# Four one-bank accumulators for dispatch, and the last batch's g in two chunk buffers

## The chip, the core and the metric

The kernel runs on one NeuronCore of a Trainium2 chip. The metric is the device time of one execution in microseconds (us), median of several runs. Of the core, TensorE (PE in the rows, PEld its weight loads), VectorE (DVE), ScalarE (ACT), GpSimd (POOL) and SyncE (SP) have queues of their own and wait for each other by semaphores; SP issues every DMA, in the order of its queue.

## The reference, cut to what matters

```python
def reference(q, k, v, moe_w_in, moe_w_out, phi, w1, w2):
    # q, k, v: (4, 12, 448, 64); causal softmax attention, per batch and head
    x = attention(q, k, v).transpose(0, 2, 1, 3).reshape(1792, 768)
    h = x @ moe_w_in                       # 768 x 2048, float64 weights
    g = np.maximum(0.01 * h, h)
    y = g @ moe_w_out                      # 2048 x 768
    logits = y @ phi                       # 1792 x 32: 8 experts of 4 slots
    d = softmax(logits, axis=0)            # dispatch: over all 1792 tokens
    slot_input = d.T @ y                   # 32 x 768
    for e in range(8):                     # w1[e]: 768 x 1024, w2[e]: 1024 x 768
        slot_out[4*e : 4*e+4] = relu(slot_input[4*e : 4*e+4] @ w1[e]) @ w2[e]
    c = softmax(logits, axis=1)            # combine
    return c @ slot_out                    # 1792 x 768, float32
```

## The kernel before, in words

Tokens are worked on in four batches of 448. Attention and the first layer are pipelined over stages: while the attention of batch b runs, `up(b - 1)` (L650) makes the 16 column tiles of g (128 of the 2048 columns each, `H` in PSUM, then `g` in SBUF) of the batch before it, and the float64 weights are converted. y is never formed: dispatch is taken as (d.T @ g) @ w_out, with w_out converted to float32 in a DRAM scratch (`wsc`), and the logits as g @ (w_out @ phi), `wprime`.

**Dispatch over batches.** The softmax over all tokens is kept running. `combine(b)` (L733) takes a batch's logits: `lt` and `pl` on PE, the new maximum `nm`, the factor `ab` by which all earlier sums shrink, `et` = exp, its transpose `dn`; then the accumulator `g_acc` (128 x 4 x 512 in PSUM, four banks, x = 0 to 3) is multiplied by `ab`, bank by bank, banks 0 and 2 on DVE, 1 and 3 on ACT (L765 to L768), and 56 calls of `mm` (L792; 112 instructions in the trace, as float32 goes in two passes) add dn.T @ g_nat. `g_nat` holds one batch's g with tokens on partitions, made by 32 x 32 transposes on DVE (`transpose_g`, L629). The batches come in the order 2, 0, 1, 3. Batch 2 goes through during stage four and only starts the accumulator, so it has nothing to rescale. Batches 0 and 1 were parked in DRAM (`g_far`) and come back through `fetch` (L710, `gb`), while `up(3)` runs; batch 3 is combined last.

**The expert weights.** `slots` (L860) is a list of places of 12 KB per partition, taken round after round by `load_next` (L891); 36 chunks of 1.5 MB go through them in this order: 4 of `wo` (from `wsc`), 16 of `w1`, 16 of `w2`. The names count down: `wo_35` to `wo_32`, `w1_31` to `w1_16`, `w2_15` to `w2_0`. The places are buffers that fall free late: 7 `wg` (the fetch buffers of batches 0 and 1), 4 `wq` (first-layer weights w16, four f each), 2 `wx` (x16 of batches 2 and 3, of which one also holds `g_spare`, batch 3's g for f < 6), and 3 `wc`, which lie where `mainp` (g_nat and batch 3's ring of five g tiles) was: 13 loads are asked for before the last combine (L908) and 3 behind it (L915). From then on each load waits until PE has used up the chunk 16 places earlier (`load_next(1)` behind each chunk's products).

**The end.** Behind the last `g_acc`: `ge` (normalised), `pgt`, `psi` (the four wo chunks), `pst`, `ph` (w1), `po` (w2), `pss`, and the output `o`. The order on each engine is set by a scheduler that works on a simulated timeline; PE's matmuls keep the written order (`in_order`, L102).

Of the kernel before, what the change touches and what calls it, by code (L numbers as in the profile page):

```python
# [10 lines left out]
F32 = mybir.dt.float32  # L11
# [23 lines left out]
def tile_attn_moe_softmoe(ctx: ExitStack, tc: tile.TileContext, q, k, v, w_in, w_out, phi, w1, w2, out, dbg=None):  # L35
# [17 lines left out]
    const = ctx.enter_context(tc.tile_pool(name="const", bufs=1))  # L53
    xpool = tc.alloc_tile_pool(name="xpool", bufs=2)
    wpool = ctx.enter_context(tc.tile_pool(name="wpool", bufs=1, side="right"))
# [15 lines left out]
    run_s = const.tile([128, 1], F32, name="run_s")  # L71
    w16 = [wpool.tile([128, 2, NP, 512], F16, name=f"w16_{i}", tag="wq", bufs=4) for i in range(4)]

# [412 lines left out]
    def columns(n):  # L486
# [15 lines left out]
        if hp == 0:  # L502
            x16[b] = xpool.tile([128, CHUNK // 2], F16, tag="x16", name=f"x16_{b}")[:, : NP * 2 * S].rearrange(
                "p (c x s) -> p c x s", c=NP, x=2
            )
# [119 lines left out]
    g_nat = None  # L625
    g_acc = [None]
    l4s = {}
# [22 lines left out]
    def up(b, before=()):  # L650
# [4 lines left out]
        if b == B - 1:  # L655
            spare = xpool.tile([128, CHUNK // 4], F32, tag="x16", name="g_spare")
        iv[b] = const.tile([128, NF], F32, tag="iv", bufs=2, name=f"iv{b}")
# [7 lines left out]
        for f in range(NF):  # L665
# [17 lines left out]
            if not far and not before and f >= group + 5:  # L683
                logits(b, group)
                group += 4
            if b == B - 1 and f < NSPARE:
                g = spare[:, S * f : S * (f + 1)]
            else:
                g = mainp.tile([128, S], F32, tag="g", bufs=GBUF if b > 1 else 3, name=f"g{b}_{f}")
            gts[b, f] = g  # L690
# [42 lines left out]
    def combine(b):  # L733
# [7 lines left out]
        def s1():  # L741
# [19 lines left out]
            if b == 2:  # L761
                nc.vector.tensor_copy(run_s, sb)
            else:
                for x in range(4):
                    if x % 2:  # L765
                        scalar.activation(g_acc[0][:, x], g_acc[0][:, x], AF.Copy, scale=ab)
                    else:
                        nc.vector.tensor_scalar(g_acc[0][:, x], g_acc[0][:, x], ab, None, ALU.mult)  # L768
            dn = mainp.tile([128, S // 32, NS], F32, tag="dn", name=f"dn{b}")
            nc.vector.transpose(dn, et.rearrange("p (c x) -> p c x", x=32))  # L770
            if b != 2:
                nc.vector.scalar_tensor_tensor(run_s, run_s, ab, sb, ALU.mult, ALU.add)
            m = const.tile([CP, NI], F32, tag="cm", bufs=1, name=f"cm{b}")
            cs = c_nat[:, NI * b : NI * (b + 1)]
            nc.vector.tensor_reduce(m, pl, AX.X, ALU.max)
            nc.vector.tensor_tensor(cs, pl, m.unsqueeze(2).to_broadcast([CP, NI, NS]), ALU.subtract)
            st.update(dn=dn)

        def s3():
            cs = c_nat[:, NI * b : NI * (b + 1)]  # L780
            scalar.activation(cs, cs, AF.Exp)
# [6 lines left out]
        def s4():  # L788
            dn, acc = st["dn"], g_acc[0]
            nb = S // 32  # L790
            for c in range(nb):
                o = 32 * (c % 4)  # L792
                for x in range(4):
                    r = slice(32 * x, 32 * x + 32)
                    mm(
                        acc[o : o + 32, x], dn[r, c], g_nat[r, c], start=b == 2 and c < 4, stop=c >= nb - 4,
                        skip_group_check=True,
                    )
# [26 lines left out]
    if True:  # L825
# [11 lines left out]
        TR[0] = 2  # L837
        mainp = tc.alloc_tile_pool(name="gring", bufs=1, reuse_waits="tile")
        pools[1] = tc.alloc_tile_pool(name="conv2", bufs=1, reuse_waits="tile")
        load_raw()  # L840
        fixed[0] = True
        for b in range(1, 4):
            if b == 3:
                tc_release(pools[1])
                tc_release(mainp)
                mainp = tc.alloc_tile_pool(name="mainp", bufs=1, reuse_waits="tile")
                pools[2] = tc.alloc_tile_pool(name="conv", bufs=1, side="right", reuse_waits="tile")
                load_raw()
                g_nat = mainp.tile([128, S // 32, DFF // 4], F32, name="g_nat")
# [7 lines left out]
        wa[0] = tc.alloc_tile_pool(name="wa", bufs=1, side="right", reuse_waits="tile")  # L857
        NQ, NX, NC = 4, 2, 3
        wc = [None]
        slots = ["wg"] * (NG - 1) + ["wq"] * NQ + ["wx"] * NX + ["wg"] + ["wc"] * NC  # L860

# [21 lines left out]
        def slot(shape, name, dtype=F32):  # L883
            where = slots[taken[0] % len(slots)]
            taken[0] += 1
            pool, tag, bufs = {
                "wg": (wa[0], "wg", NG), "wq": (wpool, "wq", NQ), "wx": (xpool, "x16", NX), "wc": (wc[0], "wc", NC),
            }[where]
            return pool.tile(list(shape), dtype, tag=tag, bufs=bufs, name=name)
# [14 lines left out]
        HB[0], TR[0] = 2, 2  # L904
        g_acc[0] = psum.tile([128, 4, 512], F32, name="g_acc")
        for _ in up(B - 1, combine(B - 2) + late):
            pass
        load_next(NQ + NG + NX)  # L908
        for step in combine(B - 1):
# [13 lines left out]
        for x in range(4):  # L923
            ge = fin.tile([128, 512], F32, tag="ge", bufs=2, name=f"ge{x}")
            if x % 2:
                nc.scalar.activation(ge, g_acc[0][:, x], AF.Copy, scale=run_s)
            else:
                nc.vector.tensor_scalar(ge, g_acc[0][:, x], run_s, None, ALU.mult)
            for k in range(4):
# [136 lines left out]

    for p in (fin, psum2, wc[0], wa[0], xpool):
        tc_release(p)
# [44 lines left out]
```

## Time and profile before

| what | value |
|---|---|
| median of 3 runs | 666.31 us (664.75 to 669.99) |
| profiled execution | 664.25 us, its span 662.3 us |
| mean granted clock of TensorE | 0.959 |
| PE busy | 582.0 us (88% of the span) |
| DVE / ACT / POOL busy | 366.6 / 291.4 / 235.5 us |
| DMA | 125.67 MB, mean 190 GB/s |

The span runs from the first to the last instruction; 1.95 us of the profiled time lie around it. Busy shares are averages over stages with different limits: the attention stages end at about 435 us, dispatch at 552 us, and the experts at 642 us.

### The profile page before, as it was taken

To read this page: it belongs to the slowest core of one execution; us is meant where nothing else is said; L and a number is where in the kernel's file an instruction comes from. 1 tells how busy PE (TensorE), PEld (TensorE's weight loads), DVE (VectorE), ACT (ScalarE), POOL (GpSimd) and SP (SyncE) were. 2 spreads that over 40 slices of the span, in tenths; PEclk is the share of its full clock that TensorE was granted. 3 is DMA by queue.
4 is the path that set the end of the run, shared out by engine and by line. 5 is a ranking of instruction groups with operands and counts; after the bars stand their busy time and mean duration, and the time that the engine had idled before them with its cause. 6 is when DMAs were issued, how large, how long until landed. Compare 5 with 4: busy or idle time off the path is not lost.

```text
span 662.3 us, 12288 instructions
## 1 busy us (share of the span) xinstructions
PE 582.0 (88%) x4836; PEld 329.6 (50%) x4836; DVE 366.6 (55%) x884; ACT 291.4 (44%) x571; POOL 235.5 (36%) x247
## 2 busy tenths in 40 slices
PE   3788889998999999999999999999989968997654
PEld 2456555554555655665555555543434434553124
DVE  5868668989955666654567566346365241001014
ACT  2677655776864656665456455411202120011013
POOL 5287952587784335542334444320000000000000
PEclk9799989998999999999999999999989997899698
DMA  9941346665642556643253222049974546999968
GB/s 186 281 117 43 84 115 175 180 165 139 196 107 76 156 179 207 187 119 95 66 142 109 84 65 81 25 157 322 349 298 179 190 191 246 423 421 424 426 253 333
DMA packets 102449, 125.67 MB, mean 190 GB/s; under 512 B 69240, under 2 KB 91256, under 8 KB 98296
## 3 DMA queue, kind: packets, MB, share of 16 engines
q1 hardware_dynamic: 102392, 124.89, 57.2%
q8 instruction: 38, 0.62, 0.4%
q14 instruction: 19, 0.16, 0.1%
HBM read 105.74 MB, written 19.14 MB: 189 GB/s over the span
## 4 chain that ended last, share of the span: by engine, by line
PE 60%; DMA 11%; DVE 10%; POOL 8%; ACT 6%; issue 3%; SPq 1%; ACTq 0%; POOLq 0%; DVEq 0%
PE H L102 26%; DMA w<-in_moe_w_dram 9%; PE O L102 5%; PE T L102 5%; PE g_acc L102 3%; PE dn L102 3%; PE S L102 2%; DVE g_nat L632 2%; PE qkps L102 2%; PE ph L971 2%; PE L L102 2%; DMA raw_i_None<-in_moe_w_in_dram 2%; PE wt_ps L102 2%; POOL w L245 2%; ACT P L113 2%
## 5 line engine op out<-in xcount | busy, mean ns | idle before, releaser
L102 PE MATMUL H<-x,w 128*128 128x448 f16 x1152 | 230.7, 355 | 0.7 <-ACT g L113 0.7
L102 PEld LDWEIGHTS <-w 128*128 128x128 f16 x1152 | 111.2, 99 | 112.4 <-issue 19.6
L396 DVE CUSTOM_DVE_ANT_0 junk<-S,mask 112x224 bf16<-112x224 f32 (+3 forms) x192 | 85.1, 443 | 60.2 <-PE S L102 57.2
L113 ACT ACTIVATE g<-H,iv 128x448 f32<-128x448 f32 x58 | 36.8, 634 | 104.2 <-PE H L102 81.1
L474 DVE RECIPROCAL rs<-rs 128x224 f32<-128x224 f32 x36 | 53.4, 1524 | 40.3 <-ACT rs L113 40.3
L113 ACT ACTIVATE P<-T 112x672 f32<-112x672 f32 (+1 forms) x72 | 56.9, 792 | 21.9 <-PE T L102 20.8
L436 POOL TENSOR_SCALAR_AFFINE_SELECT P<-P 112x448 f32<-112x448 f32 x48 | 31.0, 647 | 90.6 <-ACT P L113 53.6
L102 PE MATMUL T<-qkt 64*112 64x336 f32 (+3 forms) x576 | 59.4, 318 | 4.3 <-ACT P L113 3.2
L102 PE MATMUL O<-P,v 112*64 112x448 f32 (+3 forms) x384 | 53.2, 418 | 4.5 <-POOL P L436 4.4
L102 PEld LDWEIGHTS T<-qkt 64*112 64x112 f32 x576 | 42.2, 177 | 14.3 <-issue 5.7
L445 POOL TENSOR_TENSOR tsum<-tsum,P 112x448 f32<-112x448 f32 (+1 forms) x48 | 47.3, 986 | 1.9
L1059 PE MATMUL po<-w,hz 128*32 128x384 f32 x256 | 28.4, 566 | 16.3 <-DMA w<-in_moe_w_dram 16.3
L102 PEld LDWEIGHTS O<-P,v 112*64 112x64 f32 x384 | 25.7, 140 | 29.9 <-issue 12.6
L963 POOL MEMSET hz<- 128x256 f32 x2 | 0.6, 311 | 111.1 <-PE g_acc L102 111.1
L441 POOL TENSOR_TENSOR tsum<-P 112x672 f32<-112x672 f32 x24 | 39.1, 1630 | 1.8
L102 PE MATMUL S<-qkt 64*112 64x224 f32 (+3 forms) x192 | 31.5, 368 | 8.4 <-DVE mxe L396 3.7
L374 DVE TENSOR_TENSOR qkt<-qkps,qkt 128x448 fp32r<-128x448 f32 x48 | 29.1, 621 | 10.0 <-ACT qkt L113 10.0
L632 DVE STREAM_TRANSPOSE g_nat<-g 128x448 f32<-128x448 f32 x26 | 16.5, 638 | 30.2 <-ACT g L113 30.2
L102 PE MATMUL T<-mr,onesr 64*112 64x448 f32 (+1 forms) x192 | 30.6, 314 | 2.9 <-ACT mr L113 2.9
L236 POOL TENSOR_TENSOR cv_i_None<-cv_i_None,cs_i_None 128x768 f32<-128x768 f32 x16 | 28.6, 1785 | 11.0 <-ACT cs_i_None L113 11.0
L113 ACT ACTIVATE mr<-mps,own 128x112 fp32r<-128x112 f32 x96 | 26.2, 360 | 14.0 <-PE mps L102 13.9
L113 ACT COPY rs<-dn 128x448 f32<-128x448 f32 x18 | 9.6, 532 | 50.3 <-PE dn L102 50.3
(174 smaller groups left out, 878.6 us busy)
## 6 DMA issues: line engine op xcount, KB each, us to landing
w<-in_moe_w_dram SPq DMA_DIRECT2D x32, 1536.0 KB
raw_i_None<-in_moe_w_in_dram SPq DMA_DIRECT2D x16, 768.0 KB
raw_o_None<-in_moe_w_out_dram SPq DMA_DIRECT2D x10, 768.0 KB
g_far<-g SPq DMA_DIRECT2D x32, 224.0 KB
gb<-g_far SPq DMA_DIRECT2D x8, 896.0 KB
wo<-wsc SPq DMA_DIRECT2D x4, 1536.0 KB
qk<-in_q_dram SPq DMA_DIRECT2D x48, 112.0 KB
qk<-in_k_dram SPq DMA_DIRECT2D x48, 112.0 KB
```

The lines of the kernel that those rows point to most:

```text
L102: op(*args, **kwargs)
L113: op(*args, **kwargs)
L236: nc.gpsimd.tensor_tensor(t, t, sg, ALU.mult)
L245: nc.gpsimd.tensor_tensor(lo, w, hi, ALU.subtract)
L374: nc.vector.tensor_tensor(st[:, j, 1], p, st[:, j, 0].bitcast(F32), ALU.subtract)
L396: nc.vector.tensor_tensor_reduce(out=junk[:, :w], in0=ps[:, a, at : at + w], in1=mask[:, S - w :], scale=-1.0, scalar=3e38, op0=ALU.add, o ...
L436: nc.gpsimd.affine_select(out=d, in_=d, compare_op=ALU.is_ge, fill=0.0, base=0, pattern=[[0, 4], [1, CP]], channel_multiplier=-1,)
L441: nc.gpsimd.tensor_tensor(tsum[:CP], p[0][:CP, :, 0, CP:], p[0][:CP, :, 1, : S - CP], ALU.add)
L445: nc.gpsimd.tensor_tensor(y, y, p[1][:CP, :, j, : S - CP * (j + 2)], ALU.add)
L474: nc.vector.reciprocal(rs[:, c : c + S // 2], rs[:, c : c + S // 2])
L632: nc.vector.transpose(g_nat[:, :, 32 * f : 32 * (f + n)].rearrange("p c (f x) -> p f c x", x=32), gts[b, f].rearrange("p (c x) -> p c x", ...
L1059: nc.tensor.matmul(po[h][32 * g : 32 * g + 32], hp[:, (t0 + t) % 8], wt[:, t, DH * h - c0 : DH * (h + 1) - c0], start=t0 + t < 4, stop=t0 ...
```

## The change

`g_acc` becomes four tiles of one bank each (`g_acc0` to `g_acc3`). In `combine`, the row maximum and subtraction for the second softmax (`cm`, `c_nat`) are written in `s3`, behind the products, instead of `s1`. The ring of g tiles gets a pool of its own (`gring2` in stage four), which is released before `up(3)`; all 16 g tiles of batch 3 lie in two chunk buffers instead, f < 6 in `g_spare0` (a new place, `wd`), the others in `g_spare1` (`wq0`, where w16 of f < 4 was), six columns of tiles, used again from f = 12. x16 no longer gives one of its two buffers to g, so `wx0` is free as soon as batch 2 is through. Each of the `wq` and `wx` buffers has a tag of its own. The places are now 1 `wx0`, 7 `wg`, `wq1`, `wd`, `wq2`, `wq3`, `wx1`, `wq0` and 2 `wc`: 14 loads before the last combine and 2 behind it, still 16 in all.

```diff
-    xpool = tc.alloc_tile_pool(name="xpool", bufs=2)
+    xpool = tc.alloc_tile_pool(name="xpool", bufs=1)
-    w16 = [wpool.tile([128, 2, NP, 512], F16, name=f"w16_{i}", tag="wq", bufs=4) for i in range(4)]
+    w16 = [wpool.tile([128, 2, NP, 512], F16, name=f"w16_{i}", tag=f"wq{i}") for i in range(4)]
...
-            x16[b] = xpool.tile([128, CHUNK // 2], F16, tag="x16", name=f"x16_{b}")[:, : NP * 2 * S].rearrange(
+            x16[b] = xpool.tile([128, CHUNK // 2], F16, tag=f"wx{b % 2}", name=f"x16_{b}")[:, : NP * 2 * S].rearrange(
...
         if b == B - 1:
-            spare = xpool.tile([128, CHUNK // 4], F32, tag="x16", name="g_spare")
+            spares.append(wd[0].tile([128, CHUNK // 4], F32, tag="wd", name="g_spare0"))
...
-            if b == B - 1 and f < NSPARE:
-                g = spare[:, S * f : S * (f + 1)]
+            if b == B - 1:
+                if f == NSPARE:
+                    spares.append(wpool.tile([128, CHUNK // 4], F32, tag="wq0", name="g_spare1"))
+                g = spares[f >= NSPARE][:, S * (f % NSPARE) : S * (f % NSPARE + 1)]
             else:
-                g = mainp.tile([128, S], F32, tag="g", bufs=GBUF if b > 1 else 3, name=f"g{b}_{f}")
+                g = ring[0].tile([128, S], F32, tag="g", bufs=GBUF if b > 1 else 3, name=f"g{b}_{f}")
...
                 for x in range(4):
                     if x % 2:
-                        scalar.activation(g_acc[0][:, x], g_acc[0][:, x], AF.Copy, scale=ab)
+                        scalar.activation(g_acc[x], g_acc[x], AF.Copy, scale=ab)
                     else:
-                        nc.vector.tensor_scalar(g_acc[0][:, x], g_acc[0][:, x], ab, None, ALU.mult)
+                        nc.vector.tensor_scalar(g_acc[x], g_acc[x], ab, None, ALU.mult)
...
                     mm(
-                        acc[o : o + 32, x], dn[r, c], g_nat[r, c], start=b == 2 and c < 4, stop=c >= nb - 4,
+                        g_acc[x][o : o + 32], dn[r, c], g_nat[r, c], start=b == 2 and c < 4, stop=c >= nb - 4,
...
         wa[0] = tc.alloc_tile_pool(name="wa", bufs=1, side="right", reuse_waits="tile")
-        NQ, NX, NC = 4, 2, 3
+        tc_release(ring[0])
+        wd[0] = tc.alloc_tile_pool(name="wd", bufs=1, side="right", reuse_waits="tile")
+        NC = 2
         wc = [None]
-        slots = ["wg"] * (NG - 1) + ["wq"] * NQ + ["wx"] * NX + ["wg"] + ["wc"] * NC
+        slots = ["wx0"] + ["wg"] * NG + ["wq1", "wd", "wq2", "wq3", "wx1", "wq0"] + ["wc"] * NC
...
-        g_acc[0] = psum.tile([128, 4, 512], F32, name="g_acc")
+        g_acc += [psum.tile([128, 512], F32, name=f"g_acc{x}") for x in range(4)]
         for _ in up(B - 1, combine(B - 2) + late):
             pass
-        load_next(NQ + NG + NX)
+        load_next(len(slots) - NC)
...
-                nc.scalar.activation(ge, g_acc[0][:, x], AF.Copy, scale=run_s)
+                nc.scalar.activation(ge, g_acc[x], AF.Copy, scale=run_s)
```

How the change moves instructions, at three places.

VectorE's queue in `combine(0)` (the rescalings are the rows that write g_acc), before:

```order
L776 TENSOR_TENSOR c_nat<-pl_5515,cm_5537 112x128
L755 TENSOR_TENSOR ab_5522<-nm_5520,run_m 128x1
L757 COPY run_m<-nm_5520 128x1
L770 STREAM_TRANSPOSE dn_5534<-et_5527 128x448
L783 TENSOR_REDUCE cs_5622<-c_nat 112x4
L768 TENSOR_SCALAR g_acc<-g_acc,ab_5522 128x512
L772 SCALAR_TENSOR_TENSOR run_s<-run_s,ab_5522,sb_5528 128x1
L784 TENSOR_SCALAR cs_5622<-cs_5622 112x4
L785 RECIPROCAL cs_5622<-cs_5622 112x4
L786 TENSOR_TENSOR c_nat<-c_nat,cs_5622 112x128
L768 TENSOR_SCALAR g_acc<-g_acc,ab_5522 128x512
```

and now:

```order
L785 TENSOR_TENSOR c_nat<-pl_5525,cm_5628 112x128
L760 TENSOR_TENSOR ab_5532<-nm_5530,run_m 128x1
L762 COPY run_m<-nm_5530 128x1
L775 STREAM_TRANSPOSE dn_5544<-et_5537 128x448
L788 TENSOR_REDUCE cs_5632<-c_nat 112x4
L773 TENSOR_SCALAR g_acc_5321<-g_acc_5321,ab_5532 128x512
L773 TENSOR_SCALAR g_acc_5323<-g_acc_5323,ab_5532 128x512
L777 SCALAR_TENSOR_TENSOR run_s<-run_s,ab_5532,sb_5538 128x1
L789 TENSOR_SCALAR cs_5632<-cs_5632 112x4
L790 RECIPROCAL cs_5632<-cs_5632 112x4
L791 TENSOR_TENSOR c_nat<-c_nat,cs_5632 112x128
```

The second rescaling (its row is the one with g_acc that stood last, behind c_nat) now follows the first at once. The subtraction from `pl`, which the diff writes into `s3`, stands ahead of `dn` in both, so that edit moves nothing here. Batch 1's and batch 3's combines have changed in the same way.

ScalarE's queue at the same place, before:

```order
L113 ACTIVATE c_nat<-c_nat 112x128
L113 ACTIVATE ab_5522<-ab_5522 128x1
L113 ACTIVATE g_acc<-g_acc,ab_5522 128x512
L113 ACTIVATE g_spare<-H_4_5541,iv_5316 128x448
L113 ACTIVATE g_acc<-g_acc,ab_5522 128x512
L113 ACTIVATE g_spare<-H_5_5617,iv_5316 128x448
```

and now:

```order
L113 ACTIVATE c_nat<-c_nat 112x128
L113 ACTIVATE ab_5532<-ab_5532 128x1
L113 ACTIVATE g_acc_5322<-g_acc_5322,ab_5532 128x512
L113 ACTIVATE g_acc_5324<-g_acc_5324,ab_5532 128x512
L113 ACTIVATE g_spare_5325<-H_4_5548,iv_5326 128x448
L113 ACTIVATE g_spare_5325<-H_5_5624,iv_5326 128x448
```

The two rescalings of ACT stand together, directly behind `ab`; the g of f = 4, which stood between them, comes behind.

SP's queue at the first chunk loads, before:

```order
L715 DMA gb6_5308<-g_far_103 128x4x448
L715 DMA gb7_5452<-g_far_103 128x4x448
L897 DMA wo_35_6016<-wsc_104 128x4x768
L897 DMA wo_34_6018<-wsc_104 128x4x768
L897 DMA wo_33_6020<-wsc_104 128x4x768
L897 DMA w1_29_6028<-in_moe2_w1_dram 128x3072
L897 DMA wo_32_6022<-wsc_104 128x4x768
L897 DMA w1_31_6024<-in_moe2_w1_dram 128x3072
```

and now:

```order
L720 DMA gb6_5315<-g_far_103 128x4x448
L906 DMA wo_35_6017<-wsc_104 128x4x768
L720 DMA gb7_5462<-g_far_103 128x4x448
L906 DMA wo_34_6019<-wsc_104 128x4x768
L906 DMA wo_33_6021<-wsc_104 128x4x768
L906 DMA wo_32_6023<-wsc_104 128x4x768
L906 DMA w1_31_6025<-in_moe2_w1_dram 128x3072
L906 DMA w1_30_6027<-in_moe2_w1_dram 128x3072
```

`wo_35` goes ahead of the last fetch (into `wx0`), and `w1_29` (place `wq0`, early) has left this stretch. The last loads ahead of and behind the last combine (`w1_22` to `w1_20` were the three of `wc`), before:

```order
L897 DMA w1_27_6032<-in_moe2_w1_dram 128x3072
L897 DMA w1_26_6034<-in_moe2_w1_dram 128x3072
L897 DMA w1_24_6038<-in_moe2_w1_dram 128x3072
L897 DMA w1_22_6135<-in_moe2_w1_dram 128x3072
L897 DMA w1_21_6137<-in_moe2_w1_dram 128x3072
L897 DMA w1_20_6139<-in_moe2_w1_dram 128x3072
L897 DMA w1_19_6186<-in_moe2_w1_dram 128x3072
```

and now:

```order
L906 DMA w1_25_6037<-in_moe2_w1_dram 128x3072
L906 DMA w1_24_6039<-in_moe2_w1_dram 128x3072
L906 DMA w1_23_6041<-in_moe2_w1_dram 128x3072
L906 DMA w1_22_6043<-in_moe2_w1_dram 128x3072
L906 DMA w1_21_6138<-in_moe2_w1_dram 128x3072
L906 DMA w1_20_6140<-in_moe2_w1_dram 128x3072
L906 DMA w1_19_6187<-in_moe2_w1_dram 128x3072
```

The names stand in nearly the same order; what differs is the place that each load takes. `w1_22` takes `wq0`, free when batch 3's last g tile has been transposed and its logits taken, and only `w1_21` and `w1_20` take `wc`.

## Rows read from the trace of the kernel before

**Rows 1.** Page, part 2: busy tenths of the DMA engines, 40 slices.

```profile
DMA  9941346665642556643253222049974546999968
```

**Rows 2.** Stretches: us, busy us by engine, granted clock, DMA share, GB/s.

```profile
510.00:530.00 20.00, 20.00 (x115) 9.43 (x112) 6.69 (x13) 3.17 (x6) 0.00 (x0) 1.00 0.43 157
530.00:550.00 20.00, 14.32 (x135) 6.59 (x146) 6.91 (x20) 3.60 (x8) 0.00 (x0) 0.84 0.40 159
575.00:600.00 25.00, 25.00 (x360) 13.18 (x348) 3.66 (x18) 2.69 (x7) 1.07 (x4) 1.00 1.01 422
```

**Rows 3.** Chain of waits from 545 us: start us, us, what.

```profile
582.39 28.76 DMA w<-in_moe_w_dram
611.21 29.51 DMA w<-in_moe_w_dram
640.76 1.50 PE po L1059 x16
```

**Rows 4.** Timeline of SP: start us, us, line, operation, xcount.

```profile
536.18 0.80 SPq L897 DMA_DIRECT2D w<-in_moe_w_dram  x2
552.03 1.28 SPq L897 DMA_DIRECT2D w<-in_moe_w_dram  x3
560.51 13.19 SPq L897 DMA_DIRECT2D w<-in_moe_w_dram  x7
```

**Rows 5.** Short stretches behind an issue, columns as in rows 2.

```profile
552.00:552.50 0.50, 0.00 (x1) 0.00 (x0) 0.39 (x1) 0.00 (x0) 0.43 (x2) 1.00 0.00 0
552.50:553.00 0.50, 0.09 (x1) 0.09 (x1) 0.36 (x1) 0.10 (x1) 0.13 (x1) 1.00 0.15 25
```

**Rows 6.** Timeline, batch 0's combine: start us, us, ... [idle before <-releaser].

```profile
470.94 3.57 PE L102 MATMUL H<-x,w 128*128 128x448 f16 x18
472.44 0.19 ACT L113 ACTIVATE ab<-ab 128x1 f32<-128x1 f32 x1
473.11 0.74 DVE L768 TENSOR_SCALAR g_acc<-g_acc,ab 128x512 f32<-128x512 f32 x1
473.89 0.66 ACT L113 ACTIVATE g_acc<-g_acc,ab 128x512 f32<-128x512 f32 x1 [1.25 <-DVE g_acc L768]
474.58 0.76 DVE L768 TENSOR_SCALAR g_acc<-g_acc,ab 128x512 f32<-128x512 f32 x1
475.37 0.66 ACT L113 ACTIVATE g_acc<-g_acc,ab 128x512 f32<-128x512 f32 x1 [0.19 <-DVE g_acc L768]
476.09 4.33 PE L102 MATMUL g_acc<-g_nat,dn 32*32 32x512 f32 x112 [1.58 <-ACT g_acc L113]
```

**Rows 7.** Waits of PE from 440 to 552 us: total, times, longest.

```profile
PE g_acc L102 <- ACT g_acc L113: 8.1, 3, 5.0
PE L L102 <- DVE l L646: 3.5, 2, 2.0
```

**Rows 8.** Timeline of DVE behind batch 0's products.

```profile
480.46 8.06 DVE L632 STREAM_TRANSPOSE g_nat<-gb 128x896 f32<-128x896 f32 x8 [5.12 <-PE g_acc L102]
```

**Rows 9.** Timeline, the last logits and batch 3's combine.

```profile
536.08 1.73 PE L102 MATMUL L<-g,wprime 128*32 128x448 f32 x8
542.25 0.75 DVE L768 TENSOR_SCALAR g_acc<-g_acc,ab 128x512 f32<-128x512 f32 x1
545.23 6.77 PE L102 MATMUL g_acc<-g_nat,dn 32*32 32x512 f32 x112 [4.96 <-ACT g_acc L113]
```

**Rows 10.** PE at batch 2's products, which wait for no rescaling.

```profile
450.61 4.33 PE L102 MATMUL g_acc<-g_nat,dn 32*32 32x512 f32 x112
```

**Rows 11.** Stretches around the last products, columns as in rows 2.

```profile
540.30:543.70 3.40, 0.00 (x0) 0.00 (x0) 3.02 (x14) 1.68 (x5) 0.00 (x0) 1.00 0.98 411
547.10:550.60 3.50, 3.50 (x82) 1.67 (x66) 0.00 (x0) 0.00 (x0) 0.00 (x0) 0.50 0.00 0
```

**Rows 12.** Timeline: ACT and DVE both reading PSUM.

```profile
529.25 0.63 ACT L113 ACTIVATE g<-H,iv 128x448 f32<-128x448 f32 x1 [3.64 <-PE L L102]
529.33 0.62 DVE L648 TENSOR_TENSOR l<-L,l 128x448 f32<-128x448 f32 x1 [3.04 <-PE L L102]
```

More of the change, by code (lines that the diff above doesn't have):

```diff
@@ L625, in tile_attn_moe_softmoe @@
     g_nat = None
-    g_acc = [None]
+    g_acc = []
+    ring = [None]
+    wd = [None]
+    spares = []
     l4s = {}
@@ L772, in s1, with s3 @@
                 nc.vector.scalar_tensor_tensor(run_s, run_s, ab, sb, ALU.mult, ALU.add)
+            st.update(dn=dn, pl=pl)
+        def s3():
+            pl = st["pl"]
             m = const.tile([CP, NI], F32, tag="cm", bufs=1, name=f"cm{b}")
@@ L776, in s1 @@
             nc.vector.tensor_tensor(cs, pl, m.unsqueeze(2).to_broadcast([CP, NI, NS]), ALU.subtract)
-            st.update(dn=dn)
-        def s3():
-            cs = c_nat[:, NI * b : NI * (b + 1)]
             scalar.activation(cs, cs, AF.Exp)
@@ L788, in s4 @@
         def s4():
-            dn, acc = st["dn"], g_acc[0]
+            dn = st["dn"]
             nb = S // 32
@@ L837, in tile_attn_moe_softmoe @@
         TR[0] = 2
-        mainp = tc.alloc_tile_pool(name="gring", bufs=1, reuse_waits="tile")
+        ring[0] = tc.alloc_tile_pool(name="gring", bufs=1, reuse_waits="tile")
         pools[1] = tc.alloc_tile_pool(name="conv2", bufs=1, reuse_waits="tile")
@@ L844, in tile_attn_moe_softmoe @@
                 tc_release(pools[1])
-                tc_release(mainp)
+                tc_release(ring[0])
                 mainp = tc.alloc_tile_pool(name="mainp", bufs=1, reuse_waits="tile")
+                ring[0] = tc.alloc_tile_pool(name="gring2", bufs=1, reuse_waits="tile")
                 pools[2] = tc.alloc_tile_pool(name="conv", bufs=1, side="right", reuse_waits="tile")
@@ L857, in tile_attn_moe_softmoe @@
         wa[0] = tc.alloc_tile_pool(name="wa", bufs=1, side="right", reuse_waits="tile")
-        NQ, NX, NC = 4, 2, 3
+        tc_release(ring[0])
+        wd[0] = tc.alloc_tile_pool(name="wd", bufs=1, side="right", reuse_waits="tile")
+        NC = 2
         wc = [None]
-        slots = ["wg"] * (NG - 1) + ["wq"] * NQ + ["wx"] * NX + ["wg"] + ["wc"] * NC
+        slots = ["wx0"] + ["wg"] * NG + ["wq1", "wd", "wq2", "wq3", "wx1", "wq0"] + ["wc"] * NC
         chunks = []
@@ L886, in slot @@
             pool, tag, bufs = {
-                "wg": (wa[0], "wg", NG), "wq": (wpool, "wq", NQ), "wx": (xpool, "x16", NX), "wc": (wc[0], "wc", NC),
-            }[where]
+                "wg": (wa[0], "wg", NG), "wq": (wpool, where, 1), "wx": (xpool, where, 1), "wc": (wc[0], "wc", NC),
+                "wd": (wd[0], "wd", 1),
+            }[where[:2]]
             return pool.tile(list(shape), dtype, tag=tag, bufs=bufs, name=name)
@@ L925, in tile_attn_moe_softmoe @@
             if x % 2:
-                nc.scalar.activation(ge, g_acc[0][:, x], AF.Copy, scale=run_s)
+                nc.scalar.activation(ge, g_acc[x], AF.Copy, scale=run_s)
             else:
-                nc.vector.tensor_scalar(ge, g_acc[0][:, x], run_s, None, ALU.mult)
+                nc.vector.tensor_scalar(ge, g_acc[x], run_s, None, ALU.mult)
             for k in range(4):
@@ L1065, in tile_attn_moe_softmoe @@
         output(products())
-    for p in (fin, psum2, wc[0], wa[0], xpool):
+    for p in (fin, psum2, wc[0], wd[0], wa[0], xpool):
         tc_release(p)
```

## The prediction

> **What bounds the kernel now.** I read the DMA line of the page first [rows 1]: the sixteen engines run at nine tenths and more in slices 35 to 38 (563 to 629 us), and at 4 or 5 tenths in slices 31 to 33 (497 to 546). The stretches say the same: share 0.43 and 0.40 from 510 to 550 us, then 1.01 at 422 GB/s [rows 2]. So the last 90 us are a stream of weights, and before it stands a stretch in which the same engines are more than half idle because no buffer is free. The chain of waits ends in that stream: from 582.39 to 640.72 it is nothing but loads of the expert weights, and PE's last products start at 640.76, when the last load has landed [rows 3]. A load is asked for when the eighth before it has landed, and 29.51 / 8 = 3.69 us; a chunk is 1536 KB, 1.573 MB, which at 422 GB/s takes 3.73. I take **3.70 us a chunk**.
>
> The stream starts behind the last dispatch products: they end at 545.23 + 6.77 = 552.0 [rows 9], and at 552.03 SP asks for three chunks at once, the first into the place of g_nat [rows 4]. The first half microsecond moves nothing, the second hardly anything [rows 5], so data flow 0.9 us after an issue into an empty queue. The 17th load is asked for at 560.51, behind the first wo chunk's products [rows 4]. From 552.9 on 23 of the 36 chunks go through without a gap: 23 x 3.70 = 85.1, to 638.0; the landing is seen 2.7 us later, which I carry over unchanged. The time is therefore set by two things: **when the last dispatch products end, and how many chunks are left then**. TensorE's 88% says little, for in the stream it waits.
>
> **Part by part.** *The rescaling.* In batch 0's combine the four banks are rescaled one after the other though two engines do it: DVE at 473.11, ACT only at 473.89 (it had `ab` at 472.63 and waited 1.25 for DVE), DVE at 474.58, ACT at 475.37, then PE at 476.09 after 1.58 idle [rows 6]. One tile of four banks makes each wait for the last. With four tiles DVE's second follows its first: 473.11 + 0.74 + 0.76 = 474.61. ACT does its two from 472.63 on, to about 473.95. PE is done with H at 474.51, so its third matmul, the first into bank 2, can start at some 474.65: 1.45 earlier. Batch 1 has the same wait: 8.1 us in three waits, less 1.58 and 4.96 [rows 6, 7, 9], is 1.56, and I take 1.45 again. In batch 3's combine DVE starts at 542.25, so 542.25 + 1.51 + 0.05 = 543.81 instead of 545.23: 1.42. Sum **4.3**. Per combine the bounds are 0 (two engines at once in PSUM take twice as long) and the 1.58 of waiting; nearest to 1.45, for the trace has such a pair: ACT's read of H and DVE's read of L overlap almost wholly at 529.3 and take 0.63 and 0.62 [rows 12]. On DVE the rows run_s to c_nat now stand behind the second rescaling; they used to fill the wait, last some 0.8 us and are needed by nobody before the normalising at 552.
>
> Does it arrive? Behind batch 0's products DVE's eight transposes wait for PE to be done with g_nat (5.12 idle, then 8.06 busy [rows 8]), and PE waits for the logits copy behind them, 2.0 at the longest [rows 7]. That path moves as a whole, and so does batch 1's. From 510 to 530 PE is busy 20.00 of 20.00 us [rows 2]: nothing else can take up the gain there, nor can the new g tiles add one. Six places instead of a ring of five make ACT's writes wait for older transposes than before.
>
> *The clock.* Batch 3's products took 6.77 us, batch 2's the same 112 instructions 4.33 [rows 9, 10]. The granted clock was 1.00 up to 543.7, while PE had been idle from 540.3 on, and 0.50 from 547.1 to 550.6 with PE busy all the time [rows 11]. The idle time before them shrinks from 4.96 to some 3.5; whether the clock then falls as before, for a shorter time or not at all, no row shows. I take **1.0** of the 2.44 between the two rows, rather less than half; bounds 0 and 2.44.
>
> *One chunk more ahead.* Now 14 loads stand before the last combine. `wx0` is free early, so wo_35 goes ahead of the last fetch, which is needed only in batch 1's last logits group; in exchange `wq0` is given late. The load that decides is w1_22: before, it was the first of the three behind the products; now it waits for batch 3's last logits, whose matmuls ended at 536.08 + 1.73 = 537.81 [rows 9]. Two loads were issued at 536.18 [rows 4]; with w1_22 they are three, through by 536.18 + 0.9 + 11.1 = 548.2, or 545.3 with the first two gains taken off, in time that is idle now. So 22 chunks are left instead of 23: **3.7**. It could be worth nothing only if the three ran into the stream, and less than 3.7 by as much as they overlap it: they are through before even the earliest end of the products (552.0 - 4.3 - 2.44 = 545.3).
>
> *One buffer less behind.* Two loads stand behind the products instead of three. They are through 0.9 + 7.4 = 8.3 us after the end of the products. The next is asked for 560.51 - 552.03 = 8.48 after it and flows at 9.38: the engines are dry for 1.08 us. Before, the third load covered that. Bounds: 0, if a better clock brings the first wo products earlier, and 3, if normalising, `pgt` and the wo products run more at the low clock; I take **-1.1**, what the row's own 8.48 gives. Behind it the loads are released faster than they move, as before.
>
> *Costing nothing.* The `s3` edit leaves the order as it is. The separate tags only name the same buffers. The tile rows of `ge` could run side by side, but `pgt` on PE is the longer one.
>
> **Sum.** 4.3 + 1.0 + 3.7 - 1.1 = 7.9 us off the profiled time of 664.25: 656.35. The median of the runs shown, 666.31, lies 2.06 above it; I forecast medians, so **658.4**.
>
> **The rivals.** *A, the forecast:* 658.4, by the bounds of its terms 655 to 660.5. Chance 0.66.
>
> *B, the clock holds and nothing runs dry.* If TensorE is not lowered before batch 3's products, they take 4.33 and the first wo products come soon enough: 4.5 + 2.4 + 3.7 = 10.6, so 655.7. For it: the idle time is a third shorter. Against it: the clock had fallen 1.5 us before the products began [rows 9, 11], so a start 1.4 us earlier falls just beside it. 0.11. The Trainium skill (TensorE: Matmul & The Clock Gate, section "HAM oscillation — how this bites in real kernels") has the rule that a long enough wait puts TensorE back to the low clock, so that the work behind it starts cold; by that rule the shorter wait is what may keep the clock up, and batch 3's rows agree with it as far as the long wait goes.
>
> *C, the rescaling gives nothing.* Either engine slows the other in PSUM, or PE waits as before, for the last of the four; then 3.7 - 1.1 = 2.6 is left: 663.7. For it: no row has two engines writing PSUM at once. Against it: rows 12, and rows 6, where ACT waits for DVE and not for PSUM. 0.14.
>
> *D, the stream starves, and the kernel is slower.* With a buffer less behind g_nat, the loads w1_19 to w1_16 hang on PE's wo products. If each is asked for only when the one before is through, it goes out into an empty queue and costs the start of 0.9 and the same again at its end, some 1.9 us. Four of these and the 1.1 are 8.7 us against the 7.9 + 1.1 that are gained without the dry time: just even; a fifth (w2_15) makes it 667.9. It decides when the wo products take over 3.7 us a chunk. Before, seven loads were asked for in 13.2 us from 560.51 on [rows 4], 1.9 each, so no. 0.05; together with other mishaps, slower by any amount is 0.06.
>
> *E, the change does not do what it says:* the four tiles lie in the same four banks, so a wait might still be shared; this is C's time. The remaining 0.03 go to losses that eat most of the gain.
>
> About 1% (6.7 us) is what a measurement of this kernel can tell from no change. A gain of over 6.7 holds in A unless dry time or a shortfall in the rescaling takes 1.2: three quarters of A, 0.49, and with B 0.60. Within 1%: the rest of A, C and E, 0.34. Slower: 0.06. The **range** is 654.5 to 664.0: it takes in B and C, each with the median's place above its profile, and leaves out D and the mishaps.
>
> **What would show it.** In batch 0's and batch 1's combine, two rescalings on DVE back to back, with ACT's beside them, and PE's wait of 1.6 gone; in batch 3's, a wait of 3.5 instead of 4.96, and the products' end near 546.7. Three loads issued near 533 to 535 and landed before that end, two issued at it, the next 8.5 later with a dry microsecond between. The first of the last eight loads to be about 8 us earlier, PE's last products near 633. Wrong it would be if PE's wait before the products stayed (C), if the DMA share fell below 0.9 for several microseconds behind 555 (D), or if attention, which the change leaves alone, took another time.

## The result, and the profile after

The changed kernel takes **658.48 us** (median; 657.63 to 658.63), the kernel before 665.80 beside it (664.75 to 669.99): ratio 0.9876, 95% interval [0.9832, 0.9919], that is 1.2% faster. The forecast was 658.4. The profiled execution after took 658.63, its span 656.9 against 662.3. I cut both spans at three marks and take the differences:

| part of the span, us | before | after | difference | forecast |
|---|---|---|---|---|
| A: start to batch 2's products | 450.61 | 451.36 | +0.75 | 0 |
| B: from there to the end of batch 3's products | 101.39 | 93.71 | -7.68 | -5.3 |
| C: from there to the last weight landing | 88.72 | 88.50 | -0.22 | -2.6 |
| D: from there to the end | 21.58 | 23.33 | +1.75 | 0 |
| span | 662.3 | 656.9 | -5.4 | -7.9 |

So the forecast time came true, but not by its terms alone: B gave more, C and D gave less, and the profile shown of before was 1.55 below its median, that of after 0.15 above.

**Part B.** Timeline of the kernel after at the combines (columns as in [rows 6]; "x2" is two instructions back to back):

```profile
471.69 3.57 PE L102 MATMUL H<-x,w 128*128 128x448 f16 x18
473.42 1.24 ACT L113 ACTIVATE g_acc<-g_acc,ab 128x512 f32<-128x512 f32 x2
473.86 1.41 DVE L773 TENSOR_SCALAR g_acc<-g_acc,ab 128x512 f32<-128x512 f32 x2
475.19 4.42 PE L102 MATMUL g_acc<-g_nat,dn 32*32 32x512 f32 x112
479.65 8.07 DVE L635 STREAM_TRANSPOSE g_nat<-gb 128x896 f32<-128x896 f32 x8 [3.65 <-PE g_acc L102]
...
488.28 0.96 PE L102 MATMUL L<-gb,wprime 128*32 128x448 f32 x8 [2.03 <-DVE l L649]
489.17 1.88 PE L102 MATMUL H<-x,w 128*128 128x448 f16 x9
...
532.08 1.73 PE L102 MATMUL L<-g_spare,wprime 128*32 128x448 f32 x8
538.24 1.41 DVE L773 TENSOR_SCALAR g_acc<-g_acc,ab 128x512 f32<-128x512 f32 x2
539.04 6.03 PE L102 MATMUL g_acc<-g_nat,dn 32*32 32x512 f32 x112 [2.78 <-DVE g_acc L773]
```

PE's waits from 440 to 552 us in the kernel after (total, times, longest):

```profile
PE L L102 <- DVE l L649: 3.5, 2, 2.0
PE g_acc L102 <- DVE g_acc L773: 2.8, 1, 2.8
```

The three waits of [rows 7] for ACT, 8.1 us, are one of 2.8 for DVE. In batch 0, PE follows H without a wait; ACT's pair takes 1.24 beside DVE's 1.41, so two engines in different PSUM banks do not slow each other (0.66 and 0.74 to 0.76 each in [rows 6]). Less the 0.75 of part A, DVE's transposes begin 1.56 earlier than in [rows 8]; batch 1 gives the same again.

Between them, part B holds a gain that no term had. The kernel before, timeline of PE near 490 us:

```profile
489.08 1.72 PE L102 MATMUL L<-gb,wprime 128*32 128x448 f32 x8 [2.03 <-DVE l L646]
490.74 2.75 PE L102 MATMUL H<-x,w 128*128 128x448 f16 x9
```

and its stretches there (columns as in [rows 2]; the granted clock is the third figure from the end, 1.00 for TensorE's 2.4 GHz and 0.50 for its low clock, 1.2 GHz):

```profile
488.00:490.00 2.00, 0.92 (x8) 0.20 (x8) 1.65 (x3) 0.00 (x0) 0.00 (x0) 0.78 1.08 453
490.00:492.00 2.00, 2.00 (x12) 0.58 (x5) 0.63 (x1) 0.00 (x0) 0.00 (x0) 0.50 1.02 412
```

Before, the clock fell there behind PE's 2.03 us wait, and the logits and H took 1.72 + 2.75 instead of 0.96 + 1.88: **1.63**. After, the same wait stands, but the clock stays. Stretches of the kernel after:

```profile
488.00:490.00 2.00, 1.72 (x13) 0.62 (x14) 1.48 (x3) 0.00 (x0) 0.00 (x0) 1.00 1.06 449
490.00:492.00 2.00, 2.00 (x15) 0.60 (x14) 0.00 (x0) 0.00 (x0) 0.00 (x0) 1.00 0.97 338
530.00:550.00 20.00, 15.66 (x173) 9.35 (x171) 7.20 (x21) 4.26 (x9) 0.56 (x2) 0.89 0.76 305
538.70:542.10 3.40, 3.06 (x50) 1.44 (x65) 1.69 (x8) 0.34 (x1) 0.00 (x0) 0.50 1.03 437
542.10:545.10 3.00, 2.97 (x78) 1.47 (x47) 0.00 (x0) 0.00 (x0) 0.00 (x0) 1.00 0.88 373
548.90:555.80 6.90, 6.12 (x41) 2.89 (x44) 0.69 (x1) 0.00 (x0) 0.00 (x0) 0.51 0.86 342
554.50:555.00 0.50, 0.50 (x8) 0.18 (x4) 0.00 (x0) 0.00 (x0) 0.00 (x0) 0.50 0.00 0
```

In batch 3 the clock is low from 538.7 to 542.1, in the first half of the products (539.04 to 545.07), and again from 548.9 to 555.8 in `pgt` and the wo products. The idle stretch from 530 to 550 is filled: DMA share 0.76 instead of 0.40 in [rows 2].

**Parts C and D.** SP of the kernel after, as [rows 4]:

```profile
532.18 1.99 SPq L906 DMA_DIRECT2D w<-in_moe_w_dram  x3
545.11 1.21 SPq L906 DMA_DIRECT2D w<-in_moe_w_dram  x2
554.13 5.11 SPq L906 DMA_DIRECT2D w<-in_moe_w_dram  x4
```

and its chain of waits, as [rows 3]:

```profile
576.65 27.36 DMA w<-in_moe_w_dram
604.07 29.50 DMA w<-in_moe_w_dram
633.61 2.79 PE po L1068 x16
636.40 2.15 PE pss L1036 x4
```

Three loads go ahead of the products' end at 539.04 + 6.03 = 545.07, two at it, the next 9.02 behind the first of these two (before, 8.48): at 554.5 to 555.0 the engines stand dry (share 0.00 in the stretches above). The last landing is at 604.07 + 29.50 = 633.57; `po` then takes 2.79 and `pss` 2.15, at half clock, against 1.50 and 1.54 before.

### The profile page after: what moved, and what is told of

It reads as the page before. It is cut to its first block, busy times and chain, and to the rows that moved or that the text cites. A ratio compares the mean times of both kernels' runs of the same rounds, so it can differ in the third digit from the quotient of the medians.

```text
span 656.9 us, 12289 instructions
## 1 busy us (share of the span) xinstructions
PE 579.3 (88%) x4836; PEld 330.5 (50%) x4836; DVE 366.5 (56%) x884; ACT 290.8 (44%) x571; POOL 235.5 (36%) x247
## 4 chain that ended last, share of the span: by engine, by line
PE 61%; DMA 13%; POOL 8%; DVE 8%; ACT 5%; issue 3%; SPq 1%; ACTq 0%; POOLq 0%; DVEq 0%
PE H L102 28%; DMA w<-in_moe_w_dram 9%; PE O L102 6%; PE T L102 4%; PE g_acc L102 3%; DVE g_nat L635 2%; PE S L102 2%; PE dn L102 2%; DMA raw_i_None<-in_moe_w_in_dram 2%; PE ph L980 2%; PE qkps L102 2%; PE L L102 2%; PE wt_ps L102 2%; POOL w L245 2%; ACT P L113 2%
## 5 line engine op out<-in xcount | busy, mean ns | idle before, releaser
L113 ACT ACTIVATE g<-H,iv 128x448 f32<-128x448 f32 x48 | 30.4, 634 | 67.8 <-PE H L102 47.4
L1068 PE MATMUL po<-w,hz 128*32 128x384 f32 x256 | 26.7, 537 | 18.3 <-DMA w<-in_moe_w_dram 18.2
L113 ACT ACTIVATE g_spare<-H,iv 128x448 f32<-128x448 f32 x16 | 10.1, 634 | 64.9 <-PE H L102 64.9
```

The costliest lines, as they stand in the source:

```text
L113: op(*args, **kwargs)
L1068: nc.tensor.matmul(po[h][32 * g : 32 * g + 32], hp[:, (t0 + t) % 8], wt[:, t, DH * h - c0 : DH * (h + 1) - c0], start=t0 + t < 4, stop=t0 ...
```

## The experiments

A to D as in the table above, from each kernel's own profiled execution (us); medians and ratios to the kernel before are of all runs. The first row is the profile shown of before, the second that of after.

| kernel | median | ratio, 95% | A | B | C | D |
|---|---|---|---|---|---|---|
| before | 665.8 | | 450.6 | 101.4 | 88.7 | 21.6 |
| changed | 658.5 | 0.9876 [0.9832, 0.9919] | 451.4 | 93.7 | 88.5 | 23.3 |
| four_tiles_alone | 662.4 | 0.9921 [0.9891, 0.9950] | 453.6 | 95.6 | 89.1 | 23.1 |
| buffers_alone | 665.1 | 0.9966 [0.9937, 0.9994] | 452.1 | 101.5 | 86.4 | 23.5 |
| one_load_behind | 662.2 | 0.9947 [0.9915, 0.9979] | 452.7 | 93.9 | 90.3 | 21.6 |
| three_loads_behind | 658.7 | 0.9872 [0.9837, 0.9908] | 455.0 | 95.2 | 86.6 | 23.5 |
| three_behind_in_order | 661.8 | 0.9923 [0.9892, 0.9954] | 453.1 | 93.9 | 89.1 | 23.1 |
| fill_front | 657.3 | 0.9856 [0.9812, 0.9901] | 451.5 | 94.3 | 86.7 | 23.3 |
| fill_tail | 658.1 | 0.9872 [0.9826, 0.9918] | 453.3 | 93.7 | 87.1 | 21.5 |
| fill_both | 655.6 | 0.9845 [0.9800, 0.9890] | 453.5 | 94.3 | 86.5 | 21.6 |
| old_s3 | 659.4 | 0.9889 [0.9854, 0.9925] | 453.6 | 94.9 | 86.7 | 23.2 |
| fill_all | 657.0 | 0.9869 [0.9826, 0.9912] | 452.7 | 92.6 | 87.8 | 21.6 |

Part A, in which PE has the same matmuls in the same order before and after, ranges over 4.3 us, and the median of before was between 665.4 and 667.2 on the occasions it was timed again. So single spans are no measure of a term of 2 us; B, C and D are, if one looks where the clock fell in each. The ratio weighs all runs against all runs, and I use it for the whole (what "the ratio is worth" is 1 less the ratio, times the median of before).

**four_tiles_alone:** the kernel before, with the accumulators alone.

```diff
-        g_acc[0] = psum.tile([128, 4, 512], F32, name="g_acc")
+        g_acc += [psum.tile([128, 512], F32, name=f"g_acc{x}") for x in range(4)]
```

> The kernel before with one edit: g_acc as four one-bank tiles; buffers and loads as before (13 loads ahead, three behind the last products). Theory (the parts add up): the products' end comes 5.3 us earlier as forecast (4.3 rescaling, 1.0 clock), up to 7.7 as the profile after has it; the stream behind it is unchanged, 23 chunks, no dry time. So 665.8 - 5.3 to 7.7 = 658.1 to 660.5. Rival 1 (the gain is all in the extra load ahead, the rescaling is covered): 665 to 666. Rival 2 (TensorE's clock takes back what the rescaling gives, in the stream's end as in the profile after, 1.75 us there): about 661 to 662.

The ratio is worth 0.79%, 5.3 us [3.3, 7.3], the median 3.4. B is 5.8 shorter, although the clock fell near 490 here too; C is as before. D is 23.1: the end ran at the low clock. Timeline of PE at batch 3:

```profile
542.88 6.23 PE L102 MATMUL g_acc<-g_nat,dn 32*32 32x512 f32 x112 [2.79 <-DVE g_acc L768]
```

The wait is the changed kernel's 2.78, with nothing else changed. The median, 662.4, is above the theory's 658.1 to 660.5 and above rival 2's time; the ratio's interval (658.5 to 662.4) reaches into both. B bears the theory out: 5.8 lies in its 5.3 to 7.7, and what the median lacks is, in this profile, the 1.5 of rival 2 at the end. Rival 1 is out. With the 2.3 of buffers_alone below, the ratios add up to 7.6, against 8.3 for the whole change.

**buffers_alone:** the changed kernel, with one tile of four banks again.

```diff
-        g_acc += [psum.tile([128, 512], F32, name=f"g_acc{x}") for x in range(4)]
+        g_acc[0] = psum.tile([128, 4, 512], F32, name="g_acc")
```

> The changed kernel with g_acc as one tile of four banks again; the loads stay as changed (14 ahead, two behind). Theory: 3.7 for the chunk less, and 1.1 to 1.6 us dry between the second and the third load behind the products, so 2.1 to 2.6 us under the kernel before: 663.2 to 663.7. Rival 1 (all the gain is here): 658 to 659. Rival 3 (the dry time eats the chunk): 665 to 666.

The ratio is worth 2.3 us [0.4, 4.2], as the theory has it; the median, 665.05, shows 0.7 only and stands where rival 3 had it. Timeline of PE at batch 3:

```profile
546.70 6.86 PE L102 MATMUL g_acc<-g_nat,dn 32*32 32x512 f32 x112 [4.96 <-ACT g_acc L113]
```

With one tile the old wait of 4.96 is back, and B is 101.5, as before to 0.1; C is 2.3 shorter. Rival 1 is out. Against rival 3 stands C, here and in the other profiles with these loads (86.4 to 87.8, and 88.5 in the one shown of after, against 88.7 to 89.1 with 23 chunks left), not the median.

**one_load_behind:**

```diff
-        NC = 2
+        NC = 1
```

> The changed kernel with one chunk buffer in g_nat's place instead of two: 14 loads ahead, one behind. Theory: the one load behind is through 4.6 us (0.9 + 3.7) after the products' end, the next flows 9.9 after it as now, so the dry time grows from 1.56 to 5.3 us: 3.7 more than the changed kernel's 658.5, so 662.2, and behind it the stream runs without a gap. Rival 3 (the dry time is covered elsewhere): 658 to 659. Rival 4 (with a buffer less the later loads starve too, each going out into an empty queue at 1.9 us): 666 and more.

662.21: the theory's time. SP behind the products' end, 540.42 + 6.22 = 546.64, and the stretches there:

```profile
546.68 0.33 SPq L906 DMA_DIRECT2D w<-in_moe_w_dram  x1
555.52 5.29 SPq L906 DMA_DIRECT2D w<-in_moe_w_dram  x4
```

```profile
552.50:553.00 0.50, 0.32 (x4) 0.20 (x8) 0.12 (x1) 0.00 (x0) 0.00 (x0) 0.50 0.00 0
553.00:556.00 3.00, 3.00 (x24) 0.91 (x20) 0.00 (x0) 0.00 (x0) 0.00 (x0) 0.50 0.00 0
558.00:564.00 6.00, 5.45 (x60) 3.33 (x56) 0.92 (x2) 0.48 (x1) 0.00 (x0) 1.00 1.01 428
```

The engines move nothing for over 3.5 us, and from 558 on everything again. C is 90.3, 3.2 to 3.9 above the 86.4 to 87.1 of most profiles with two loads behind. What a load less behind costs is the dry time and nothing later: rival 4, the starving stream, is out, even with one buffer in g_nat's place where there were three before.

**three_loads_behind** was meant to move one load behind the products:

```diff
-        slots = [... "wq2", "wq3", "wx1", "wq0"] + ["wc"] * NC
+        slots = [... "wq2", "wq3", "wx1"] + ["wc"] * NC + ["wq0"]
-        load_next(len(slots) - NC)
+        load_next(len(slots) - NC - 1)
-        load_next(NC)
+        load_next(NC + 1)
```

> The changed kernel with one load moved: 13 loads ahead, and three behind the products (the load into the last w16 tile's place is asked for behind the two into g_nat's place). Theory: 23 chunks are left instead of 22, 3.7 more, and the dry 1.56 is gone, so 2.1 above the changed kernel: 660.6. Rival 3 (no dry time that counts): 3.7 above, 662.2. Rival 5 (a load more ahead is worth nothing, because it only shifts the queue): 656.9 to 658.5.

It did not do so: the scheduler put that load ahead of the two it was written behind, three went out from 535.76 on as in the changed kernel, and C is 86.6. It says nothing on its question and, as every engine has the same instructions in the same order, is one more sample of the changed kernel: 658.74. The second try ties the load to the issue before it:

```diff
+        loaded_last()
+        with tc.issue_after(last_load[0]):
+            load_next(1)
```

> As three_loads_behind, with the order of the loads kept: 13 loads ahead, and the third, into the last w16 tile's place, asked for behind the two into g_nat's place. Theory: 23 chunks left, no dry time; from the products' end to the first landing of the last load some 87.0 us, as in the kernel before and with four tiles alone (87.0, 86.9), against 84.9 of the changed kernel: 660.6. Rival (no dry time that counts): 88.6, 662.2. Rival (the load ahead is worth nothing): 83.4 to 84.9, 657 to 658.5.

SP issued two, three and four loads now, the three at the products' end, 546.91:

```profile
533.86 0.80 SPq L906 DMA_DIRECT2D w<-in_moe_w_dram  x2
546.94 1.46 SPq L906 DMA_DIRECT2D w<-in_moe_w_dram  x3
555.83 5.24 SPq L906 DMA_DIRECT2D w<-in_moe_w_dram  x4
```

The first landing of the last load is 87.0 after the products' end (547 to 634.0), the theory's number; C is 89.1, as with four tiles alone and 2.0 to 2.7 above the 86.4 to 87.1 of most profiles with two loads behind. The median rose by 3.3, to 661.8, nearer to the 662.2 of the rival without dry time than to 660.6; the ratio rose by 0.5%. What decides between them is the landing, 87.0 and not 88.6. So the chunk ahead is worth its 3.7, less the dry time.

**fill_front, fill_tail, fill_both** ask whether the clock falls because PE waits. They add matmuls whose results nobody reads.

```diff
+            if b == B - 1:
+                fill(11)      # in s1, behind pl: 128x128 matmuls of istack and ident
...
+            if 8 <= x < len(pieces) - 1:
+                fill(8, "h", 4)      # behind the products of w2 chunk x
```

> The changed kernel with eleven 128x128 matmuls of no use on PE between batch 3's last transposing products (pl) and its dispatch products, some 2.4 us of the 2.78 that PE waits there. Theory (the clock falls because of this wait): the clock stays at 1.00, the products take about 4.4 instead of 6.03 to 6.23, pgt and the first wo products run at the full clock too, which also brings the next load up to 1.5 us earlier: 1.7 to 3.2 under the changed kernel's 658.5, so 655.3 to 656.8. Rival (the clock falls whatever PE does there, from the narrow products themselves): the fill runs low, 4.7 us, and delays the products by 2: 659 to 660.5.

Timeline of PE and two stretches of fill_front:

```profile
537.83 2.70 PE L102 MATMUL fill<-ident,istack 128*128 128x128 f32 x22
540.78 4.95 PE L102 MATMUL g_acc<-g_nat,dn 32*32 32x512 f32 x112 [0.24 <-DVE g_acc L786]
```

```profile
538.70:542.10 3.40, 3.15 (x52) 2.26 (x52) 3.03 (x12) 2.04 (x6) 0.00 (x0) 1.00 1.02 434
552.30:555.80 3.50, 3.50 (x32) 1.15 (x28) 0.00 (x0) 0.00 (x0) 0.00 (x0) 0.66 1.01 355
```

With the wait filled the products take 4.95, in all three kernels that have the fill, against 6.03 to 7.51 in the seven that have four tiles without it. The rival is out for this place. B hides it in this execution, because the clock fell near 490 again; in fill_all, where it did not, B is 92.6. The median, 657.3, lies 0.5 above the theory's range, and the ratio's interval overlaps that of the changed kernel: a gain in time is not shown.

> The changed kernel with eight 128x128 matmuls of no use on PE behind each of the w2 chunks 8 to 14, about 1.7 us of the 2.1 to 2.3 that PE waits for each. Theory: the low clock at the end comes from PE's idle time in the stream; with it filled, the last products take 1.50 instead of 2.79 and pss 0.9 instead of 1.5, and from the last landing to the end 21.6 us instead of 23.3: 656.8. Rival (the narrow products call the low clock, not the idle time): the fill runs low and takes 3.4, with the products 6.2 of the 3.7 us per chunk, PE falls behind and the end is later by up to 2.5 x 3: 660 to 666.

Last rows of PE and a stretch, first of fill_tail:

```profile
631.94 2.05 PE L102 MATMUL fill<-ident,istack 128*128 128x128 f32 x16
634.11 1.50 PE L102 MATMUL po<-w,hz 128*32 128x384 f32 x16
635.74 0.88 PE L1049 MATMUL pss<-so,istack 128*128 128x384 f32 x2
```

```profile
631.00:636.00 5.00, 4.75 (x48) 2.73 (x38) 0.56 (x1) 0.33 (x1) 0.00 (x0) 1.00 0.20 82
```

and of the kernel after:

```profile
630.02 2.79 PE L1068 MATMUL po<-w,hz 128*32 128x384 f32 x16 [2.13 <-DMA w<-in_moe_w_dram]
633.61 2.79 PE L1068 MATMUL po<-w,hz 128*32 128x384 f32 x16 [0.81 <-DMA w<-in_moe_w_dram]
636.33 1.56 PE L1036 MATMUL pss<-so,istack 128*128 128x384 f32 x2
```

```profile
627.40:634.00 6.60, 3.66 (x25) 0.88 (x24) 0.00 (x0) 0.00 (x0) 0.00 (x0) 0.50 0.44 181
```

D is 21.5 to 21.6 in all three executions with this fill; without it 23.1 to 23.5 in seven of nine. The two others, the profile of before and one_load_behind, had their low stretch earlier in the stream (612 to 625 and 610 to 625 us), where PE waits for loads anyhow. So the 1.8 us are part of most profiles, with one tile or four, old buffers or new; one_load_behind, with the change in it, lacks them as the profile shown of before does, so that their absence there is no mark of the kernel before. That the fill is what saves them is likely and not shown: in all three executions with it the clock also fell once near 608 to 612 us, at the first filled chunk (in fill_tail it is 0.50 from 610 to 612, and 1.00 from 614 on), and the two executions without the fill that fell early were at 1.00 at the last landing as well. The median gained 0.3 of the 1.7 forecast; that it is a gain is not shown. The rival, 660 and more, is out.

> Both fills together. Theory: 1.7 to 3.2 in front and 1.7 at the end under the changed kernel: 653.6 to 655.1. Rival: as the worse of the two alone, 660 and more.

655.56, ratio 0.9845: the fastest median here, 2.9 under the changed kernel, but 0.5 above the theory's range, and the intervals overlap: that it beats the changed kernel is not shown.

**old_s3** undoes the edit of `s3` (the subtraction of the maxima goes back into `s1`).

```diff
-        def s3():
-            pl = st["pl"]
             m = const.tile([CP, NI], F32, tag="cm", bufs=1, name=f"cm{b}")
...
+        def s3():
```

> The changed kernel with the s3 edit undone. The instructions of PE, DVE and ACT stand in the same order with it and without, so this is a second look at the changed kernel. Theory: 658.5; the time from batch 2's products to the end of batch 3's is 93.7 to 95.4 (the upper where the clock falls near 490 us as it did in the kernel before), from there to the last load's first landing 84.3 to 84.9, from the last landing to the end 21.5 or 23.3, by where the clock is. Rival (the edit takes DVE's work out of the wait): 1 to 2 us more, with a later rescaling on DVE.

659.36, 0.9 above the changed kernel, and B, the first landing (84.3) and D as expected. PE's wait before the products is 2.78 here too, so the rival's later rescaling is not there. With the same instructions in the same order as the changed kernel, batch 3's products took 7.23 here and 6.03 there: how much of them falls into the low clock differs from execution to execution.

**fill_all** is fill_both with two more fills, on the two sides of `pgt`.

> As fill_both, with three more 128x128 matmuls of no use on PE before pgt (it waits 0.85 there) and three before psi (0.78). Theory: the clock, which still fell to 0.62 to 0.66 near 552 to 556 with both fills, holds there too; the first wo products end 0.7 earlier, and so the next load is issued that much earlier and the dry time is 0.8 instead of 1.5: from the products' end to the last load's first landing 83.5 instead of 84.2, and 654.8 instead of 655.6 in the median. Rival (the clock falls there because of the narrow pgt and psi products): no change, or 0.3 more, 655.6 to 655.9.

```diff
+        fill(3)      # once ahead of the pgt matmuls, once behind them
```

The rival holds as to the clock, though not as to its cause; the median, 657.0, is above both forecasts, and by the ratio, 0.9869 against the 0.9845 of fill_both, there is no gain. Stretch of fill_all:

```profile
548.90:552.30 3.40, 3.34 (x21) 2.91 (x24) 0.69 (x1) 0.00 (x0) 0.00 (x0) 0.58 0.98 405
552.30:555.80 3.50, 3.50 (x24) 0.98 (x20) 0.00 (x0) 0.00 (x0) 0.00 (x0) 0.50 0.66 267
```

PE has no wait before 552, and the clock falls all the same, during `pgt` and the fill behind it. There the engine is busy with weight loads (2.91 of 3.40) and products 32 columns wide; a wait of the engine is not the cause in this place. The Trainium skill (TensorE: Matmul & The Clock Gate, section "A second HAM failure mode: psum-queue depth-cycling") has the clock swing where PE idles briefly between groups of matmuls; this run shows it with those pauses filled, so what did it here stays open.

## Why the prediction was right

*The rescaling, 4.3.* Right, and slightly small: 1.56 in batch 0, 1.56 in batch 1. For batch 3, from the last logits to the products' end takes 15.92 before, with 2.44 of that lost to the clock, so 13.48 at the full one; fill_front, with the clock up, takes 11.92. That is 1.56 again, **4.7** together. PE even starts on the first bank while the others are still being rescaled, so that its wait is 2.78 instead of the 3.5 forecast, and the products last 4.95 at full clock instead of 4.33.

*The clock of the last products, 1.0.* Measured 2.93 - 1.56 = 1.4 in this pair of executions, within the bounds. But the term was a draw, not a size: the products took 6.03 to 7.51 without the fill, where 4.95 is the full clock. Against the 2.44 that the shown execution of before lost, that makes the term -0.1 to 1.4, and 0.9 on the mean of the seven. Rival B's condition, a clock that holds through the shorter wait, did not come about in any execution without the fill. The rule of the Trainium skill that was quoted with it (TensorE: Matmul & The Clock Gate, section "HAM oscillation — how this bites in real kernels": a long enough wait puts TensorE back to the low clock) agrees with fill_front as far as this wait goes: clock 1.00 with the wait filled, 0.50 without.

*What the forecast lacked in B.* The 1.63 near 490. From batch 0's to batch 1's products it is 27.10 in both profiles with one tile, 25.55 in three with four tiles and 23.92 to 23.93 in seven: 1.55 is the rescaling, 1.63 the clock behind the 2.03 wait. Whether four tiles make the fall rarer, two of two against three of ten can't say.

*The chunk ahead, 3.7, and the dry time, -1.1.* The mechanism is shown by one_load_behind and three_behind_in_order. The dry time goes with the clock, as the forecast's bound of 3 had it. In the shown pair the next load came 9.02 after the two at the products' end, not 8.48, since `pgt` and the first wo products ran low (548.9 to 555.8); 9.02 + 0.9 - 8.3 makes 1.6 by the forecast's own sum, so 2.1 instead of 2.6. The first part of the last load bears it out: it lands 84.9 behind the products' end, against 87.0 before. In fill_front, fill_both, old_s3 and three_loads_behind the next load came 8.4 behind the products' end and that first part landed at 84.2 to 84.3: 2.7, the forecast's size. To the last landing, C is 86.4 to 87.1 in six of the other seven profiles with these loads (87.8 in fill_all, whose next load came 9.5 behind the products), against 88.7 to 89.1 with 23 chunks left. In the profile shown, C is 88.5, because there the last of the sixteen parts of each load lands 3.6 us behind the first; in the other profiles that is 1.7 to 2.5, as read at the last load. The spread grows in single steps and then stays. Behind the dry time, each step of 0.4 us or more, in all twelve traces, falls into a load during which the DMA engines also fetched 16 KB of instructions, about 1 us each time (in the kernel after from 2.2 to 3.7, with a fetch at 573.8 us). That one of the sixteen engines falls behind by its fetches is the likely reason; the records do not name the engine, so it is not shown.

*The sum.* In the shown pair B's surplus of 2.4 was eaten by A's 0.75, C's late parts and D's 1.75, none of which goes with the change in the other profiles. Over all profiles B is 94.4 (mean of seven with four tiles and no front fill) against 101.4 and 101.5, C some 2 less: about 9, and the ratio's 8.3 us [5.4, 11.2] holds that and the forecast's 7.9. That 658.4 met the median within 0.1 is luck; that it lay within 2 is not.

*The rivals.* C and E fell with four_tiles_alone, D with one_load_behind. Of the signs named beforehand, most came: back to back rescalings, the gone waits, loads from 532.18 and at 545.11, the dry microsecond, last products at 633.61. The products' end, 545.07, and the three loads came earlier than named (546.7; 533 to 535). Two were drawn badly: "attention takes another time" does not speak against the change, since part A moves by up to 4.3 us in kernels that are alike there, and the wait of 3.5 came out shorter for a good reason.

## What to carry over

Give an accumulator that two engines rescale one tile per bank, if it is the tile that waits are counted by; the gain was what the rows of the old waits showed, to 0.2 us each. When a kernel ends in a stream, count the chunks left when the stream can start, and the time until the next buffer comes free, and subtract: both terms came out of single rows, the second to half a microsecond, by where the clock fell. And before comparing two profiles, cut them at marks and look where the clock fell in each: 1.6 to 1.8 us here came and went between executions of kernels that are alike in that place.

## What the runs showed of the hardware

- The clock fell behind waits of 2.03 (in five of twelve executions) and 2.78 us (in seven of seven without the fill), and also where PE hardly waited (fill_all). Useless matmuls in the wait of 2.78 held it in three of three. At the last landing of the stream it was 1.00 in three of three with eight behind each chunk, and in two of nine without.
- Two engines working at once in two banks of PSUM ran at their single speed: 1.24 for ACT's two, 1.41 for DVE's.
- The sixteen parts of one 1.5 MB load land 1.7 to 3.6 us apart at the stream's end, and PE's last products wait for the last of them (633.57, start at 633.61).
